# Attention scores of eight heads at once on parts of the array, in a kernel of attention, soft mixture of experts and a gated layer

## The chip, the cores and the metric
The kernel runs on one core of one Trainium2 chip. The metric is the device time of one execution in microseconds (us). The engines named below are TensorE (PE: matrix products; its weight loads are listed apart as PEld), VectorE (DVE), ScalarE (ACT), GpSimd (POOL) and SyncE (SP, which issues the DMAs).

## The reference, cut to what matters
All arrays are float32: 8 batches, 8 heads, 576 tokens, head size 64, 32 packing queries `p` per head.

```python
def sm_attn(qq, kk, vv):
    s = scale * (qq @ kk.T)
    a = exp(s - max(s)); a = a / (sum(a) + 1e-9)
    return a @ vv
p_packed = sm_attn(p, k, v)            # 32 x 64 per head
out = sm_attn(q, p_packed, p_packed)   # 576 x 64 per head
x = out, tokens x (heads * 64)         # 4608 x 512
# soft mixture of experts: logits = x @ phi (32 slots), softmax over tokens
# (dispatch) and over slots (combine); eight experts relu(s @ w1) @ w2
# gated layer: (sigmoid(x @ w_gate) * (x @ w_val)) @ w_out
```

## The kernel before, in words
The host lays `q` and `k` out by pairs of heads: 128 rows are the 64 head elements of two heads, and there are four pairs, j = 0 to 3. So row half r of pair j belongs to head 2j + r.

The attention stage (lines 107 to 526) runs a software pipeline over the eight batches. Iteration i of the loop at line 522 does the steps of the list `order`, each on batch i - lag: on batch i the packing scores (`scores`), their exponentials' transposes (`scores_tail`, `scores_t`) and the product with v (`pack`); on batch i - 1 the query scores (`pack_t`, `query`, `query_t`); on i - 2 to i - 4 the second softmax's sums, the attention's transposes, the slot logits with their running maximum, and the products that collect the slots (`dispatch`, `dispatch_t`, `slots_in`). Iterations 4 to 7 hold all lags; 0 to 3 fill the pipeline, 8 to 11 empty it.

The scores of both kinds are made by `heads_mm` (line 188). One call takes four heads (g = 0 or 1): two pairs, two halves of 288 tokens. The stationary operand is 128 rows by 64 columns: the packing queries of both heads of a pair in a block-diagonal layout with zeros (tiles `ptd` and `ppt`), so that one product gives two heads' scores. The two pairs of a call lie on two column parts of the array (`tile_position` (0, 0) and (0, 64)). The result goes to one buffer `sp` of two PSUM banks; the pool `p_big` has two such buffers, used by calls in turn. `scores` takes the maximum on VectorE (line 210) and the exponential with its sum on ScalarE (211); `query` copies the block to `s2`, group 0 on VectorE (the name s20 is in `ON_VECTOR`), group 1 on ScalarE. `packing` (157) writes the scaled block-diagonal `ptd` for the next batch on GpSimd.

Transposes go to PSUM buffers of the pool `p_tr` (two), the small products to `p_sm` (two). A step that needs a buffer waits until the last reader of its previous content is through.

What sets the order: the framework's planner orders every engine's instructions of the attention stage by its own costs, with the order of the text as priority, so TensorE's calls can be cut by others. The later stages are written with `keep_in_program_order` (class `Ordered`, line 550), which pins an engine's instruction behind the one written before it.

Loads go through SP's queue in order: p, then k, v, q of each batch, then the expert weights `wt` into 14 slots as these come free. The rest of the expert weights goes to slots that come free after the attention stage. The experts (line 732 on) begin with products that need `prun`, the attention's last result, and the gated layer follows.

Of the kernel before, what the change touches and what calls it, by code (L numbers as in the profile page):

```python
# [44 lines left out]
ON_VECTOR = {"m2", "s20"}  # L45
# [3 lines left out]
def kernel(  # L49
# [22 lines left out]

    ident = const.tile([128, 128], F32, name="ident")
    make_identity(nc, ident)
    i4 = const.tile([128, NS], F32, name="i4")
    masks = const.tile([128, 2, 2], F32, name="masks")
    nc.gpsimd.memset(masks, 0.0)
    for q in range(4):
        r = slice(32 * q, 32 * q + 32)
        nc.gpsimd.tensor_copy(out=i4[r, :], in_=ident[r, r])  # L80
        nc.gpsimd.memset(masks[r, 0, q % 2 : q % 2 + 1], 1.0)
        nc.gpsimd.memset(masks[r, 1, q // 2 : q // 2 + 1], 1.0)
# [19 lines left out]
    a4 = att.enter_context(tc.tile_pool(name="a4", bufs=4))  # L102
# [6 lines left out]
    ptds = [a1.tile([128, 4, 2, NP], F32, name=f"ptd{i}") for i in range(2)]  # L109
    phi = a1.tile([128, 4, NS], F32, name="phi")  # L110
    for t in ptds:
        nc.gpsimd.memset(t, 0.0)
# [44 lines left out]
    def packing(b):  # L157
        for r in range(2):
            rows = slice(64 * r, 64 * r + 64)
            (nc.gpsimd if b else nc.vector).tensor_scalar_mul(  # L160
                out=ptds[b % 2][rows, :, r, :], in0=praw[rows, b], scalar1=0.125
            )

    nc.sync.dma_start(out=praw, in_=pd)
    packing(0)
    for b in range(B):
        load(kt, b, kd[b], "kt")
        if b == 0:
            nc.sync.dma_start(out=phi, in_=phid)
        load(vt, b, vd[b], "vt")  # L170
        load(qt, b, qd[b], "qt")
# [16 lines left out]
    def heads_mm(dst, lhs, rhs, g):  # L188
        for n in range(2):
            for i in range(2):  # L190
                j = 2 * g + i
                nc.tensor.matmul(  # L192
                    dst[64 * i : 64 * i + 64, n, 0:HS],
                    lhsT=lhs[:, j].rearrange("p r k -> p (r k)"),
                    rhs=rhs[:, S * j + HS * n : S * j + HS * n + HS],
                    start=True,
                    stop=True,
                    tile_position=(0, 64 * i),
                )

    def scores(b, g):
        w = st.setdefault(b, {})
        if g == 0:
            w["nmax"] = a2.tile([128, 2], F32, name="nmax")
            w["ssum"] = a2.tile([128, 2], F32, name="ssum")
            w["e1"] = a1.tile([128, 2, S], F32, name="e1")
        sp = p_big.tile([128, 2, 512], F32, name="sp", tag="big")
        heads_mm(sp, ptds[b % 2], kt[b], g)
        nm = w["nmax"][:, g : g + 1]
        nc.vector.tensor_reduce(out=nm, in_=sp[:, :, 0:HS], axis=AX.XY, op=ALU.max, negate=True)  # L210
        nc.scalar.activation(  # L211
            w["e1"][:, g, :].rearrange("p (n s) -> p n s", n=2),
            sp[:, :, 0:HS],
            AF.Exp,
            bias=nm,
            accum_out=w["ssum"][:, g : g + 1],
        )
        if g == 1 and b + 1 < B:
            packing(b + 1)

    def scores_t(b, g):
        w = st[b]
        if g == 0:
            w["e1t"] = a1.tile([128, 8, 128], F32, name="e1t")
        tp = p_tr.tile([128, 4, 128], F32, name="tp", tag="tr")
        for c in range(4):
            nc.tensor.transpose(tp[:, c, :], w["e1"][:, g, 128 * c : 128 * c + 128], ident)
        copy(f"e1t{g}", w["e1t"][:, 4 * g : 4 * g + 4, :], tp)

    def scores_tail(b):  # L230
        w = st[b]
        e1, ssum = w["e1"], w["ssum"]
        tp = p_tr.tile([128, 4, 128], F32, name="tp", tag="tr")
        nc.tensor.transpose(tp[:, 0, :], e1[:, 1, 448:S], ident)
        nc.tensor.transpose(tp[0:64, 0, :], e1[:, 0, 512:S], ident)
        for g in range(2):
            rows = slice(64 * g, 64 * g + 64)
            copy(f"etail{g}", etail[rows, g, :], tp[rows, 0, :])
        nc.gpsimd.tensor_scalar_add(out=ssum, in0=ssum, scalar1=EPS)
        rs = a2.tile([128, 2], F32, name="rs")  # L240
        nc.vector.reciprocal(out=rs, in_=ssum)
        rsm = w["rsm"] = a2.tile([128, 2, 2], F32, name="rsm")
        nc.gpsimd.tensor_tensor(
            out=rsm,
            in0=rs[:, :, None].to_broadcast([128, 2, 2]),
            in1=masks[:, 0:1, :].to_broadcast([128, 2, 2]),
            op=ALU.mult,
        )

    def pack(b):  # L250
        w, v = st[b], vt[b]
        pq = p_sm.tile([128, 512], F32, name="pq", tag="sm")
        for g in range(2):
            for c in range(5):
                for q in range(4):
                    d0 = 64 * (4 * g + q)
                    if c < 4:
                        lhs, rhs = w["e1t"][:, 4 * g + c], v[:, DM * c + d0 : DM * c + d0 + 64]
                    else:
                        lhs, rhs = etail[:, g], v[:, 4 * DM + 64 * q : 4 * DM + 64 * q + 64]  # L260
                    nc.tensor.matmul(
# [7 lines left out]

        pp = w["pp"] = a4.tile([128, 2, 2, D], F32, name="pp")  # L270
        nc.vector.tensor_tensor(
            out=pp,
            in0=pq[:, 0:128].rearrange("p (g d) -> p g d", g=2)[:, :, None, :].to_broadcast([128, 2, 2, D]),
            in1=w["rsm"][:, :, :, None].to_broadcast([128, 2, 2, D]),
# [3 lines left out]
    def pack_t(b):  # L278
        w = st[b]
        pq = p_sm.tile([128, 512], F32, name="pq", tag="sm")  # L280
        for g in range(2):
            nc.tensor.transpose(pq[:, 128 * g : 128 * g + 128], w["pp"][:, g].rearrange("p r d -> p (r d)"), ident)
        ppt = w["ppt"] = a2.tile([128, 4, 2, NP], F32, name="ppt")
        copy("ppt", ppt.rearrange("p j r k -> p (j r k)"), pq[:, 0:256])

    def pack_phi(b):
        w = st[b]
        pq = p_sm.tile([128, 512], F32, name="pq", tag="sm")
        for j in range(4):
            g, i = j // 2, j % 2  # L290
            nc.tensor.matmul(
                pq[64 * i : 64 * i + 64, NS * g : NS * g + NS],
                lhsT=w["ppt"][:, j].rearrange("p r k -> p (r k)"),
                rhs=phi[:, j],
                start=True,
                stop=True,
                tile_position=(0, 64 * i),
# [4 lines left out]
    def query(b, g):  # L302
        w = st[b]
        if g == 0:
            w["s2"] = a1.tile([128, 2, S], F32, name="s2")
        sp = p_big.tile([128, 2, 512], F32, name="sp", tag="big")
        heads_mm(sp, w["ppt"], qt[b], g)
        copy(f"s2{g}", w["s2"][:, g, :].rearrange("p (n s) -> p n s", n=2), sp[:, :, 0:HS])

    def query_t(b, *parts):  # L310
        w = st[b]
        tps = []
        for c0, nch in parts:
            tp = p_tr.tile([128, 16, NP], F32, name="tp", tag="tr")
            for ci in range(nch):
                t0 = TOK[c0 + ci]
                for g in range(2):
                    h0 = 8 * ci + 4 * g
                    nc.tensor.transpose(  # L319
# [33 lines left out]
    def attn_t(b, part):  # L353
# [5 lines left out]
        if part < 2:  # L359
            for c in range(4):  # L360
                nc.tensor.transpose(tp[:, c, :], w["a"][:, c, 128 * part : 128 * part + 128], ident)
            copy(f"at{part}", at[:, part, 0:512].rearrange("p (c t) -> p c t", c=4), tp)
        else:
            for g in range(2):
                nc.tensor.transpose(tp[:, g, :], w["a"][:, 4, 128 * g : 128 * g + 128], ident)
            copy("at2", at[:, :, 512:S], tp[:, 0:2, 64:128])

    def logits(b):
        w = st[b]
        lp = p_sm.tile([128, 512], F32, name="lp", tag="sm")  # L370
        for g in range(2):
            for c in range(4):
                nc.tensor.matmul(
# [7 lines left out]
        for g in range(2):  # L381
            nc.tensor.matmul(
# [14 lines left out]
    def logits_t(b):  # L397
# [3 lines left out]
        nc.tensor.transpose(lt[:, 0:128], ls[:, 0:128], ident)  # L401
        nc.tensor.transpose(lt[:, 128:160], ls[0:32, 128:256], ident[0:32, 0:32])
        nc.tensor.transpose(lt[:, 256:384], cm.to_broadcast([128, 128]), ident)
# [18 lines left out]
    def dispatch(b):  # L422
        w = st[b]
        tps = p_sm.tile([128, 512], F32, name="tps", tag="sm")
        for c in range(4):
            nc.tensor.matmul(
# [8 lines left out]
        for c in range(4):  # L435
            n = slice(64 * c, 64 * c + 64 + c // 3)
            nc.tensor.matmul(
# [14 lines left out]
    def dispatch_t(b):  # L452
        w = st[b]
        tt = p_tr.tile([128, 512], F32, name="tt", tag="tr")
        for g in range(2):
            nc.tensor.matmul(
# [3 lines left out]
        tts = w["tts"] = a2.tile([128, 2, 2, NS], F32, name="tts")  # L460
        nc.vector.tensor_tensor(
            out=tts,
            in0=tt[:, 0 : 2 * NS].rearrange("p (g s) -> p g s", g=2)[:, :, None, :].to_broadcast([128, 2, 2, NS]),
            in1=masks[:, 1:2, :, None].to_broadcast([128, 2, 2, NS]),
# [11 lines left out]
    def slots_in(b):  # L476
        w = st.pop(b)
        pps = p_sm.tile([128, 512], F32, name="pps", tag="sm")
        for k in range(4):
            g = k // 2  # L480
            nc.tensor.matmul(
                pps[32 * k : 32 * k + 32, 0:128],
                lhsT=w["tts"][:, g, k % 2, :],
                rhs=w["pp"][:, g].rearrange("p r d -> p (r d)"),
                start=True,
                stop=True,
                tile_position=(0, 32 * k),
            )
# [6 lines left out]

    order = [
        (0, scores, 0),
        (3, attn_t, 1),
        (1, pack_t),
        (2, query_sum, (0, 2)),  # L500
        (3, attn_t, 2),
        (2, query_t, (4, 1)),
        (2, query_sum, (2, 2)),
        (0, scores, 1),
        (0, scores_tail),
        (0, scores_t, 0),
        (4, dispatch),
        (1, query, 0),
        (3, logits),
        (1, query, 1),  # L510
        (4, dispatch_t),
        (3, logits_t),
        (0, scores_t, 1),
        (2, query_sum, (4, 1)),
        (2, pack_phi),
        (1, query_t, (0, 2)),
        (1, query_t, (2, 2)),
        (4, slots_in),
        (0, pack),
        (2, attn_t, 0),  # L520
# [27 lines left out]


    class Ordered:  # L550
        def __init__(self, engine):
            self.engine = engine

        def __getattr__(self, name):
            op = getattr(self.engine, name)
            return lambda *args, **kw: tc.keep_in_program_order(op(*args, **kw))  # L556

    pe, act, dve, pool = [Ordered(e) for e in (nc.tensor, nc.scalar, nc.vector, nc.gpsimd)]
# [513 lines left out]
```

## Time and profile before

| | us |
|---|---|
| median of 3 runs | 568.49 (565.71 to 568.69) |
| the profiled execution | 568.5 |
| its span, first to last instruction | 566.7 |
| mean granted TensorE clock | 0.988 |

The span is the time from the first to the last instruction of the profiled execution; 1.8 us of its device time lie around it. The clock is the share of full speed that TensorE was granted.

### The profile page before, as it was taken

The numbers are of one execution on the slowest core, as the hardware profiler recorded it, in microseconds if no ns is written. First come the engines' busy times: TensorE is split into PE (matmuls) and PEld (weight loads), VectorE is DVE, ScalarE is ACT, GpSimd is POOL, SyncE is SP. The second block draws the span as 40 slices with busy tenths as digits, with TensorE's granted clock in tenths as the row PEclk, the third lists the DMA queues.
The fourth block names the chain that finished last, engine by engine and source line by source line (L and its number), as shares of the span: only waits on it lengthen the run. The fifth ranks groups of instructions, "written<-read, shape, count | busy, mean of one in ns | idle before, by whom it ended". The sixth has DMA issues, their size and how long they took to land.

```text
span 566.7 us, 10833 instructions
## 1 busy us (share of the span) xinstructions
PE 534.4 (94%) x4177; PEld 407.3 (72%) x4177; DVE 345.0 (61%) x846; ACT 292.6 (52%) x749; POOL 52.2 (9%) x131
## 2 busy tenths in 40 slices
PE   3889999997989799999999999999999999999997
PEld 1556666655555567787688888888888888888885
DVE  1377777783446478988989456567444644464444
ACT  2356555542356478897695444444444544454443
POOL 4132221230010000111011000000000000000000
PEclk9899999996999999999999999999999999999999
DMA  8999999931998656235200002022000200020002
GB/s 350 423 419 418 421 419 421 361 129 53 391 418 338 242 223 223 92 132 224 75 1 1 2 10 102 0 113 113 0 1 0 112 1 2 0 112 1 1 1 112
DMA packets 18099, 91.46 MB, mean 161 GB/s; under 512 B 1792, under 2 KB 2176, under 8 KB 11520
## 3 DMA queue, kind: packets, MB, share of 16 engines
q1 hardware_dynamic: 18048, 90.77, 40.6%
q8 instruction: 33, 0.54, 0.4%
q14 instruction: 18, 0.15, 0.1%
HBM read 81.33 MB, written 9.44 MB: 160 GB/s over the span
## 4 chain that ended last, share of the span: by engine, by line
PE 64%; DVE 3%; ACT 2%; DMA 2%; issue 1%; DVEq 0%
PE o_ps L556 50%; PE qg L556 11%; PE so_ps L556 2%; DMA wt<-in_w_dram 2%; PE qa L556 1%; ACT wgv L556 1%; DVE u L556 1%; DVE gv L556 1%; DVE held L556 0%; ACT gh L556 0%; ACT gv L556 0%; DVE gst L556 0%; DVE gl L556 0%; DVE wl L556 0%; ACT cst L556 0%
## 5 line engine op out<-in xcount | busy, mean ns | idle before, releaser
L556 PE MATMUL o_ps<-wh,gh 128*128 128x512 f32 x432 | 171.4, 397 | 1.6 <-DVE held L556 0.8
L556 PE MATMUL o_ps<-wl,gh 128*128 128x512 f32 x432 | 170.6, 395 | 0.0
L556 DVE TENSOR_TENSOR gv<-gv,qg 128x256 f32<-128x256 f32 x216 | 90.6, 419 | 131.2 <-ACT gv L556 130.4
L556 PE MATMUL o_ps<-wh,gl 128*128 128x512 f32 x432 | 168.3, 390 | 0.0
L556 ACT ACTIVATE gv<-qg 128x256 f32<-128x256 f32 x216 | 82.9, 384 | 155.7 <-PE qg L556 155.7
L556 PEld LDWEIGHTS qg<-cst,gst 128*128 128x128 f32 x432 | 79.5, 188 | 24.3 <-DVE gv L556 5.2
L556 PEld LDWEIGHTS o_ps<-wh,gl 128*128 128x128 f32 x432 | 81.2, 188 | 18.8 <-DVE gl L556 0.3
L556 PEld LDWEIGHTS o_ps<-wh,gh 128*128 128x128 f32 x432 | 81.1, 188 | 13.3 <-ACT gh L556 2.2
L556 DVE TENSOR_TENSOR gl<-gv,gh 128x256 fp32r<-128x256 f32 x216 | 90.5, 419 | 0.2
L556 PE MATMUL qg<-cst,gst 128*128 128x256 f32 x432 | 87.7, 285 | 2.6 <-DVE gv L556 1.6
L556 ACT CAST gh<-gv 128x256 fp32r<-128x256 f32 x216 | 86.6, 401 | 6.8 <-DVE gv L556 6.1
L556 PEld LDWEIGHTS o_ps<-wl,gh 128*128 128x128 f32 x432 | 81.9, 190 | 8.9
L192 PE MATMUL sp<-kt,ptd 128*64 128x288 f32 x128 | 23.2, 443 | 7.5 <-DMA kt<-in_k_dram 7.5
L556 ACT ACTIVATE wgv<-wgv 128x1024 f32<-128x1024 f32 (+3 forms) x28 | 28.3, 1021 | 0.0
L346 POOL TENSOR_TENSOR a<-ex,sm 128x512 f32<-128x512 f32 (+1 forms) x24 | 21.6, 904 | 67.9 <-DVE sm L345 49.6
L556 POOL CAST gst<-gst 32x128 fp32r<-32x128 f32 x40 | 13.5, 339 | 136.9 <-issue 66.1
L331 ACT ACTIVATE ex<-ex 128x512 f32<-128x512 f32 (+1 forms) x24 | 13.3, 560 | 16.9 <-DVE ex L328 16.9
L192 PE MATMUL sp<-qt,ppt 128*64 128x288 f32 x128 | 19.1, 419 | 1.7 <-ACT e L211 1.7
L192 PEld LDWEIGHTS sp<-kt,ptd 128*64 128x64 f32 x128 | 9.7, 145 | 14.6 <-issue 11.2
L324 DVE TENSOR_REDUCE mx<-tp 128x16 f32<-128x512 f32 (+1 forms) x24 | 14.2, 597 | 8.1 <-PE tp L319 7.6
L211 ACT ACTIVATE e<-sp,nmax 128x576 f32<-128x576 f32 x16 | 11.9, 745 | 13.2 <-DVE nmax L210 13.1
L556 PE MATMUL so_ps<-wt,htz 128*32 128x256 f32 x256 | 17.0, 384 | 1.1 <-DVE htz L556 1.0
(154 smaller groups left out, 575.4 us busy)
## 6 DMA issues: line engine op xcount, KB each, us to landing
wt<-in_w_dram SPq DMA_DIRECT2D x26, 1152.0 KB, 10.5
kt<-in_k_dram SPq DMA_DIRECT2D x8, 1152.0 KB, 22.3
vt<-in_v_dram SPq DMA_DIRECT2D x8, 1152.0 KB, 22.3
qt<-in_q_dram SPq DMA_DIRECT2D x8, 1152.0 KB, 22.4
out_dram<-os SPq DMA_DIRECT2D x35, 256.0 KB, 2.1
wgv<-in_wg_dram SPq DMA_DIRECT2D x5, 1024.0 KB, 7.0
wgv<-in_wv_dram SPq DMA_DIRECT2D x5, 1024.0 KB, 7.7
wo<-in_wo_dram SPq DMA_DIRECT2D x5, 1024.0 KB, 5.0
```

Of the source, the lines that this page charges most:

```text
L192: nc.tensor.matmul(dst[64 * i : 64 * i + 64, n, 0:HS], lhsT=lhs[:, j].rearrange("p r k -> p (r k)"), rhs=rhs[:, S * j + HS * n : S * j + H ...
L211: nc.scalar.activation(w["e1"][:, g, :].rearrange("p (n s) -> p n s", n=2), sp[:, :, 0:HS], AF.Exp, bias=nm, accum_out=w["ssum"][:, g : g ...
L324: nc.vector.tensor_reduce(out=mx[:, 0:n], in_=tp[:, 0:n, :], axis=AX.X, op=ALU.max)
L331: nc.scalar.activation(ex, ex, AF.Exp, scale=0.125)
L346: nc.gpsimd.tensor_tensor(out=w["a"][:, c0 : c0 + nch, 0:256].rearrange("p c (h k) -> p c h k", k=NP), in0=exs[c0][:, 0:n, 0:NP].rearrange ...
L556: return lambda *args, **kw: tc.keep_in_program_order(op(*args, **kw))
```

## The change
`heads_mm` now makes the scores of all eight heads in one call. A matmul takes one head: 64 rows (row half r) by 32 columns (part j), so eight parts of the array hold eight heads; the heads of row half r go to buffer r of two `sp` buffers, both taken by the call. With that the heads are grouped by their place in the pair (r) and no longer by halves of the list. The zero-padded `ptd`, `packing` and the masked `rsm` go; `p` is scaled in place once; `phi` is laid out with zeros, in two DMAs after a memset; `pp` and `ppt` have half the columns; `tts` has twice the columns, `slots_in` eight narrower products instead of four; `scores_tail` has four transposes instead of two. The copy s20 moves to ScalarE. Every TensorE instruction of the stage is pinned to the written order, and `order` is rewritten; VectorE, ScalarE and GpSimd stay with the planner. `room` only keeps the addresses of later tiles.

```diff
-ON_VECTOR = {"m2", "s20"}
+ON_VECTOR = {"m2"}
...
+    pe, act, dve, pool = [Ordered(e) for e in (nc.tensor, nc.scalar, nc.vector, nc.gpsimd)]
...
-    a4 = att.enter_context(tc.tile_pool(name="a4", bufs=4))
+    a4 = att.enter_context(tc.tile_pool(name="a4", bufs=5))
...
+    phi = a1.tile([128, 4, 2, NS], F32, name="phi")
+    nc.gpsimd.memset(phi, 0.0)
+    a1.tile([128, 384], F32, name="room")
...
-    packing(0)
+    nc.vector.tensor_scalar_mul(out=praw[:, 0], in0=praw[:, 0], scalar1=0.125)
+    nc.gpsimd.tensor_scalar_mul(out=praw[:, 1:B], in0=praw[:, 1:B], scalar1=0.125)
...
-    def heads_mm(dst, lhs, rhs, g):
-        for n in range(2):
-            for i in range(2):
-                j = 2 * g + i
-                nc.tensor.matmul(
-                    dst[64 * i : 64 * i + 64, n, 0:HS],
-                    lhsT=lhs[:, j].rearrange("p r k -> p (r k)"),
-                    rhs=rhs[:, S * j + HS * n : S * j + HS * n + HS],
...
-                    tile_position=(0, 64 * i),
+    def heads_mm(dst, lhs, rhs):
+        for n in range(2):
+            for j in range(4):
+                for r in range(2):
+                    rows = slice(64 * r, 64 * r + 64)
+                    pe.matmul(
+                        dst[r][32 * j : 32 * j + 32, n, 0:HS],
+                        lhsT=lhs[rows, j, :],
+                        rhs=rhs[rows, S * j + HS * n : S * j + HS * n + HS],
...
+                        tile_position=(64 * r, 32 * j),
...
+        sps = [p_big.tile([128, 2, 512], F32, name="sp", tag="big") for _ in range(2)]
+        heads_mm(sps, praw[:, b], kt[b])
+        for g, sp in enumerate(sps):
...
+            pe.transpose(tp[:, g, :], e1[:, g, 448:S], ident)
+            pe.transpose(tp[0:64, g, :], e1[:, g, 512:S], ident)
...
     order = [
-        (0, scores, 0), (3, attn_t, 1), (1, pack_t), (2, query_sum, (0, 2)),
-        (3, attn_t, 2), (2, query_t, (4, 1)), (2, query_sum, (2, 2)),
-        (0, scores, 1), (0, scores_tail), (0, scores_t, 0), (4, dispatch),
-        (1, query, 0), (3, logits), (1, query, 1), (4, dispatch_t),
-        (3, logits_t), (0, scores_t, 1), (2, query_sum, (4, 1)),
-        (2, pack_phi), (1, query_t, (0, 2)), (1, query_t, (2, 2)),
-        (4, slots_in), (0, pack), (2, attn_t, 0),
+        (0, scores), (4, dispatch), (1, pack_t), (3, attn_t, 1),
+        (2, query_sum, (0, 2)), (2, query_sum, (2, 2)), (3, attn_t, 2),
+        (2, query_t, (4, 1)), (1, query), (3, logits), (2, pack_phi),
+        (4, dispatch_t), (0, scores_tail), (0, scores_t, 0),
+        (0, scores_t, 1), (3, logits_t), (2, query_sum, (4, 1)),
+        (0, pack), (4, slots_in), (2, attn_t, 0),
+        (1, query_t, (0, 2)), (1, query_t, (2, 2)),
     ]
```

## Rows read from the trace of the kernel before

**Rows 1.** The page: busy time of each engine, share of the span, instructions.

```profile
PE 534.4 (94%) x4177; PEld 407.3 (72%) x4177; DVE 345.0 (61%) x846; ACT 292.6 (52%) x749; POOL 52.2 (9%) x131
```

**Rows 2.** Windows of the attention stage, every engine; the heading names the columns.

```profile
core 0: us, PE busy (x) PEld busy (x) DVE busy (x) ACT busy (x) POOL busy (x), PEclk, DMA share, GB/s
7.47:18.27 10.80, 8.10 (x108) 5.45 (x108) 2.11 (x4) 3.35 (x8) 1.47 (x4) 0.84 1.01 423
18.27:29.54 11.27, 9.69 (x144) 5.92 (x144) 5.94 (x11) 5.68 (x13) 1.47 (x4) 1.00 1.01 420
29.54:41.10 11.56, 10.37 (x149) 6.50 (x145) 7.99 (x19) 6.28 (x15) 4.15 (x7) 1.00 1.02 422
41.10:53.14 12.04, 11.81 (x171) 7.38 (x170) 9.20 (x21) 7.19 (x20) 4.18 (x7) 1.00 1.01 418
...
57.07:71.65 14.58, 14.57 (x205) 9.08 (x204) 10.35 (x29) 8.22 (x23) 4.24 (x9) 1.00 1.02 423
...
101.04:111.93 10.89, 10.73 (x185) 7.37 (x184) 8.13 (x22) 6.06 (x17) 1.22 (x5) 1.00 0.93 359
111.93:119.78 7.85, 7.85 (x88) 4.68 (x87) 5.85 (x21) 3.46 (x12) 2.82 (x4) 1.00 0.59 197
119.78:128.54 8.76, 7.30 (x86) 4.56 (x82) 8.12 (x25) 5.26 (x15) 2.71 (x3) 1.00 0.20 82
128.54:137.76 9.22, 6.40 (x79) 3.53 (x79) 3.48 (x15) 2.04 (x9) 0.00 (x0) 0.75 0.01 2
```

**Rows 3.** Timeline of TensorE, 67.38 to 72.6: start, us, what.

```profile
67.39 1.19 PE L192 MATMUL sp<-kt,ptd 128*64 128x288 f32 x8
68.51 0.66 PE L361 MATMUL tp<-ident,a 128*128 128x128 f32 x4
...
69.53 0.70 PE L192 MATMUL sp<-kt,ptd 128*64 128x288 f32 x2
70.16 0.44 PE L319 MATMUL tp<-ident,s 128*128 128x128 f32 x2
70.53 1.19 PE L192 MATMUL sp<-kt,ptd 128*64 128x288 f32 x6
71.65 0.64 PE L426 MATMUL tps<-a,ee 128*32 128x257 f32 x8
...
72.46 0.46 PE L192 MATMUL sp<-qt,ppt 128*64 128x288 f32 x2
```

**Rows 4.** Timeline of all engines, 136.5 to 138.5.

```profile
138.22 0.58 PE L556 MATMUL qa<-i 128*128 128x128 f32 x1 [0.47 <-DVE prun L490]
138.33 0.33 SPq L143 DMA_DIRECT2D wt<-in_w_dram  x1
```

**Rows 5.** Windows of line 192 alone (the head products).

```profile
67.38:67.68 0.30, 0.29 (x2) 0.20 (x4) 1.00 1.02 430
```

**Rows 6.** Groups by shape in 67.39 to 81.97: busy us, mean ns.

```profile
L211 ACT ACTIVATE e<-sp,nmax 128x576 f32<-128x576 f32 x2 | 1.5, 756 | 0.0
L210 DVE TENSOR_REDUCE nmax<-sp 128x1 f32<-128x576 f32 x2 | 1.5, 754 | 0.2 <-PE sp L192 0.2
L324 DVE TENSOR_REDUCE mx<-tp 128x16 f32<-128x512 f32 x2 | 1.4, 692 | 0.3 <-PE tp L319 0.2
L328 DVE TENSOR_TENSOR ex<-tp,mx 128x512 f32<-128x512 f32 x2 | 1.3, 681 | 0.0
...
L186 ACT COPY at<-tp 128x512 f32<-128x512 f32 x2 | 1.2, 576 | 0.7 <-PE tp L361 0.7
L186 ACT COPY s<-sp 128x576 f32<-128x576 f32 x1 | 0.6, 638 | 0.5 <-PE sp L192 0.5
...
L186 ACT COPY etail<-tp 64x128 f32<-64x128 f32 x2 | 0.5, 259 | 1.0 <-PE tp L235 1.0
L211 ACT ACTIVATION_READ_ACCUMULATOR e<-sp,nmax 128x1 f32 x2 | 0.4, 213 | 0.0
```

More of the change, by code (lines that the diff above doesn't have):

```diff
@@ L168 @@
         if b == 0:
-            nc.sync.dma_start(out=phi, in_=phid)
+            for r in range(2):
+                rows = slice(64 * r, 64 * r + 64)
+                nc.sync.dma_start(out=phi[rows, :, r, :], in_=phid[rows])
         load(vt, b, vd[b], "vt")
@@ L201, in scores @@
-    def scores(b, g):
-        w = st.setdefault(b, {})
[L203 to L219, printed above, removed]
+            for j in range(4):
+                for r in range(2):
+                    rows = slice(64 * r, 64 * r + 64)
+                    pe.matmul(
+                        dst[r][32 * j : 32 * j + 32, n, 0:HS],
+                        lhsT=lhs[rows, j, :],
+                        rhs=rhs[rows, S * j + HS * n : S * j + HS * n + HS],
+                        start=True,
+                        stop=True,
+                        tile_position=(64 * r, 32 * j),
+                    )
@@ L280, in pack_t @@
         pq = p_sm.tile([128, 512], F32, name="pq", tag="sm")
[L281 to L284, printed above, removed]
+        pe.transpose(pq[:, 0:128], w["pp"].rearrange("p r d -> p (r d)"), ident)
+        ppt = w["ppt"] = a2.tile([128, 4, NP], F32, name="ppt")
+        copy("ppt", ppt.rearrange("p j k -> p (j k)"), pq[:, 0:128])
     def pack_phi(b):
@@ L300, in pack_phi, with query @@
         copy("m2", m2.rearrange("p g s -> p (g s)"), pq[:, 0 : 2 * NS])
-    def query(b, g):
+    def query(b):
         w = st[b]
[L304 to L308, printed above, removed]
+        w["s2"] = a1.tile([128, 2, S], F32, name="s2")
+        sps = [p_big.tile([128, 2, 512], F32, name="sp", tag="big") for _ in range(2)]
+        heads_mm(sps, w["ppt"], qt[b])
+        for g, sp in enumerate(sps):
+            copy(f"s2{g}", w["s2"][:, g, :].rearrange("p (n s) -> p n s", n=2), sp[:, :, 0:HS])
     def query_t(b, *parts):
@@ L496 @@
     order = [
-        (0, scores, 0),
+        (0, scores),
+        (4, dispatch),
+        (1, pack_t),
         (3, attn_t, 1),
-        (1, pack_t),
         (2, query_sum, (0, 2)),
+        (2, query_sum, (2, 2)),
         (3, attn_t, 2),
         (2, query_t, (4, 1)),
-        (2, query_sum, (2, 2)),
-        (0, scores, 1),
+        (1, query),
+        (3, logits),
+        (2, pack_phi),
+        (4, dispatch_t),
         (0, scores_tail),
         (0, scores_t, 0),
[L507 to L511, printed above, removed]
+        (0, scores_t, 1),
         (3, logits_t),
-        (0, scores_t, 1),
         (2, query_sum, (4, 1)),
-        (2, pack_phi),
+        (0, pack),
+        (4, slots_in),
+        (2, attn_t, 0),
         (1, query_t, (0, 2)),
         (1, query_t, (2, 2)),
-        (4, slots_in),
-        (0, pack),
-        (2, attn_t, 0),
     ]
```

137 lines of the change are left out of this document (63 added, 74 removed).

## The prediction
> **What bounds the kernel now.** I read the page first: TensorE is busy for 534.4 of 566.7 us, VectorE for 345.0, ScalarE for 292.6 [rows 1]. That is a mean over stages, so the windows come next, cut where an iteration's score products start (up to 53.14) and, from 57.07, where its dispatch products start [rows 2]. In a full iteration (three such windows, 57.07 to 101.04, 14.5 to 14.8 us each) TensorE is busy for 14.57 of 14.58 us at a granted clock of 1.00, VectorE for 10.35, ScalarE for 8.22. The transfers run at a share of 1.0 there, but TensorE waits for none: they run ahead into the expert weights, and from 111.93 they thin out to 0.59, 0.20 and 0.01. So in the attention stage TensorE's own stream is the bound. Third, the timeline of one iteration [rows 3], which shows how that stream is cut: blocks of one array shape behind each other. Fourth, the end of the stage [rows 4]: the experts' first product waits for the last `prun`, and the weight transfers that had stopped start again beside it, at 138.33. So what the stage gains, all behind it gains: 138.22 to 566.7 us is carried over unchanged, and so are the 1.8 us between span and profiled time (568.5, which is the median too).
>
> **Step 1, the head products.** A call of heads_mm took 1.12 us (67.39 to 68.51) [rows 3]. Its four matmuls show as eight passes (x8) on two column parts, so four rounds. From the transposes between the calls: eight take 1.02 us (68.51 to 69.53), two take 0.37 (70.16 to 70.53), so one costs 0.11 and a block of a new shape 0.15; a round is then (1.12 - 0.15) / 4 = 0.24 us. Afterwards a call has 16 matmuls, 32 passes, on eight parts: four rounds again, for eight heads and not four. I add 0.05 for starting eight parts: 1.17 us. Two calls a batch in place of four: 4.48 - 2.34 = 2.14 us saved. That two column parts run at once is in these rows; that two row halves do is in none. Bounds: eight rounds a call if the halves take turns (2.1 us, nothing saved), or 2.24 saved if the start is free. I take the column parts' behaviour, the nearest row.
>
> In the rows the weight load of a part's next pass is not held up: in the first 0.30 us of a call two passes began and four loads were already done [rows 5]. The Trainium skill (TensorE: Matmul & The Clock Gate, Part 3, "The mechanism") says that loads overlap running matmuls only where the row group differs; by it each later round would wait for its load, which is rival D. The trace contradicts it here.
>
> **Step 2, the written order.** The second score call was cut by two transposes: 69.53 to 71.65 less their 0.37 is 1.75 us, 0.63 more than a whole call. That goes. Besides the head calls the iteration has 14 blocks of one shape in the timeline (attn_t with pack_t, query_t three times, dispatch in two shapes, logits twice, scores_tail with scores_t, dispatch_t to the second scores_t, pack_phi, slots_in twice, the second with pack, attn_t 0); the new order has 7 (dispatch on 128 rows, dispatch on 64, nine transposes, logits with pack_phi, the transposes from dispatch_t to logits_t, pack with slots_in, the last twelve transposes). 7 x 0.15 = 1.05 us saved. Small edits cancel: pack_t loses a transpose (-0.11), scores_tail gains two (+0.22), pack_phi runs on four parts instead of two (0 to -0.2), slots_in has the same columns in more pieces. TensorE's own work: 14.57 - 2.14 - 0.63 - 1.05 = 10.75 us.
>
> **Step 3, the other engines.** VectorE loses the copy s20 (some 0.7 us; pp halves, tts doubles): about 9.8 us. ScalarE gains it (0.64): 8.8. Both stay under 10.75, so no total becomes the bound; the chains between the engines do, because a call now takes both score buffers at once and TensorE may no longer go round a wait.
>
> **Step 4, walking one full iteration.** T = 0 is the start of the score products, done at 1.2.
> - VectorE still has the maximum and subtraction of the last two query_t blocks (0.69, 0.68; one each 0.6 when queued [rows 6]). The second block's transposes end at 0, so VectorE is through at 1.9. Then two score maxima of 0.75 (0.67 apart): 2.6 and 3.3.
> - ScalarE: the exponentials of the scores take 0.76 and 0.21 for the sum: 2.7 to 3.6, and 3.6 to 4.4 when both buffers are free. On the same queue lie the query exponential (0.63), ts, ppt, and the copy at1 (0.58), which must be out before query_t(4,1) finds its buffer; those transposes stand ahead of the query products. Behind the score exponentials that makes 5.3 to 5.7, ahead of some 4.6.
> - TensorE alone would reach the query products at 3.1: 1.17, dispatch 0.81 (71.65 to 72.46), nine transposes 1.1. So it waits for 1.5 to 2.6 us; I take 2.1. All behind it on TensorE waits too; nothing can fill the hole.
> - After the query products ScalarE has s20 and s21 (0.64 each), the ls copies and two etail (0.26 each) ahead of e1t, while TensorE needs only some 1.5 us to come to the second scores_t: 0.2 us of waiting. The last query_t block needs at0's buffer (0.58 behind four transposes, 0.44 of other work): 0.3 us more.
> An iteration is 10.75 + 2.1 + 0.5 = 13.4 us (12.4 with the short chain, 14.5 if the copies queue badly).
>
> **Step 5, the sum.** Steady part: from the first full iteration's scores (53.14) to the first dispatch without scores (111.93) are 58.79 us. The new order puts dispatch right after scores, so these are four iterations: 4 x 13.4 = 53.6, -5.2. Start, against rows 2: iteration 0 (10.80, clock 0.84) -2.0, an estimate: one call of two goes (1.1 us, more at the lower clock), and the next scores no longer stand behind pack_t's wait for pp. For the others the walk of step 4 is repeated with the steps that they have: iteration 1 (11.27) has no backlog of query reductions, so the query products go at 3.8, and 9.7 in all, -1.6; iteration 2 (11.56) has the backlog, query products at 4.4, 11.0, -0.6; iteration 3 (12.04) has the at copies too, 12.3, +0.3. Drain: 7.85 becomes 8.0 (+0.1, one query call saved against the strict order); 8.76, of which TensorE is idle 1.46, -1.5; the last 9.22 is a chain of dispatch and copies, 0. The new phi zeroing and second phi DMA on SP's queue lie in the 7.47 us in which TensorE waits for the first keys; nothing. Scaling p on GpSimd once replaces scaling per batch, which was off the chain. Sum: -5.2 steady, -3.9 start, -1.4 drain: -10.5. 568.5 - 10.5 = 558.0 us.
>
> **Rivals.**
> A. The waits of step 4 don't come, because VectorE takes the score maxima ahead of the query reductions: an iteration is TensorE's 10.75. 58.8 - 43.0 = 15.8, start 6.5, drain 2.5: 544 us. For it: VectorE has 4 us to spare in each of these windows [rows 2]. Against: the two buffers, both filled by each call.
> B. The row halves take turns: 8 rounds a call. An iteration is 13.4 + 2 x 0.97 = 15.3 us, steady +2.6, start about +2.5 (each of three iterations loses 1.9 against the forecast), drain +0.9: 574 us, slower. It decides from about 0.7 us a call lost. For it: no row shows two row halves at once. Against: column parts do run at once.
> C. The chain is longer: at1, e1t and the score exponentials queue so that an iteration is 14.5 us. Steady -0.8, start -1.5, drain 0: 566 us. For it: VectorE and ScalarE follow their own order, which TensorE's written one doesn't know.
> D. The loads of a part's next pass wait until the running pass is through. A pair's loads take 0.1 us (0.20 for four [rows 5]); three later rounds in each of two calls make 0.6 a batch, 5 us over eight: 563. Against: the same row. The sentence of the Trainium skill in step 1 is for it.
>
> **How the numbers follow.** Forecast 0.59, A 0.18, C 0.12, B 0.07, D 0.04. The forecast's own range is 552 to 564 (the iteration 12.4 to 14.5, start and drain within 2). To hold eight times in ten it reaches into A and to C: 545 to 567; outside lie B and the far end of A. Within 0.5% (2.8 us, about what a measurement of this kernel can tell) lie most of C and the edge of the forecast: 0.10. Slower by more: B and a still longer chain, 0.08. Faster: 0.82.
>
> **What would show it.** Right: a call on eight parts near 1.2 us with 32 passes; windows of full iterations at 13 to 14 us in which TensorE, for the first time, waits before the query products for ScalarE's e or at; ScalarE near 9 us an iteration; the experts' first product near 128. Wrong: a call of 2 us (B), iterations under 12 (A) or over 14.3 (C), or an expert stage that does not begin earlier by what the attention stage saved.

## The result and the profile after

| | median of the runs shown | range | profiled execution | span |
|---|---|---|---|---|
| before | 567.91 us (8) | 565.71 to 568.98 | 568.5 | 566.7 |
| after | 573.01 us (8) | 570.16 to 576.68 | 570.5 | 568.7 |

The ratio is 1.0102, 95% interval 1.0063 to 1.0140: one per cent slower, where 558.0 us was forecast and 567 was the upper end. The two profiled executions are 2.0 us apart, and that is the stage: the experts' first product begins at 140.38 us (before 138.22 [rows 4]), and from it to the end are 428.3 us (before 428.5). Its row, from the timeline:

```profile
140.38 1.01 PE L79 MATMUL qa<-i 128*128 128x128 f32 x3 [0.47 <-DVE prun L487]
```

The other 3 us between the medians go with the granted clock: the mean clock of a run is 0.970 to 0.988 after and 0.984 to 0.994 before, and the slowest run after (576.68) has 0.970, the fastest (570.16) 0.988.

The page of after, engine line (answers to [rows 1]):

```profile
PE 519.8 (91%) x4505; PEld 400.6 (70%) x4505; DVE 339.2 (60%) x837; ACT 295.7 (52%) x757; POOL 45.5 (8%) x105
```

Windows of after, cut at the starts of the score products and, from 111.80, of the dispatch products (columns and cuts as in [rows 2]):

```profile
core 0: us, PE busy (x) PEld busy (x) DVE busy (x) ACT busy (x) POOL busy (x), PEclk, DMA share, GB/s
7.43:16.23 8.80, 6.95 (x124) 4.42 (x125) 1.58 (x3) 3.25 (x8) 0.22 (x1) 1.00 1.01 420
16.23:25.97 9.74, 7.40 (x173) 4.59 (x165) 2.50 (x6) 4.58 (x11) 0.22 (x1) 1.00 1.01 421
25.97:37.65 11.68, 8.72 (x180) 5.37 (x179) 7.50 (x18) 6.55 (x15) 2.89 (x4) 1.00 1.01 417
37.65:52.17 14.52, 12.34 (x210) 7.67 (x209) 8.75 (x21) 8.35 (x21) 2.93 (x4) 0.88 1.02 422
...
66.70:81.20 14.50, 11.91 (x245) 7.98 (x244) 10.32 (x28) 8.62 (x23) 3.04 (x5) 1.00 1.01 421
81.20:97.30 16.10, 13.52 (x245) 8.81 (x244) 10.47 (x28) 8.74 (x23) 3.05 (x5) 0.89 1.01 418
...
111.80:121.60 9.80, 7.98 (x121) 5.03 (x120) 8.07 (x23) 5.30 (x15) 2.78 (x4) 1.00 0.60 228
121.60:129.50 7.90, 5.47 (x80) 3.54 (x79) 6.89 (x23) 3.92 (x11) 2.40 (x3) 1.00 0.00 0
129.50:140.40 10.90, 7.43 (x102) 4.45 (x102) 4.01 (x16) 2.78 (x11) 0.32 (x1) 0.75 0.01 2
```

A full iteration is as long as before (14.5 us), with TensorE busy for 11.91 us in place of 14.57. Two of the iterations have a granted clock under 0.9 (the end of the stage is low in both kernels). Finer windows show the stretches at the lower of the two levels, 1.2 GHz:

```profile
42.80:46.20 3.40, 3.38 (x57) 1.85 (x58) 1.35 (x6) 1.50 (x3) 2.21 (x4) 0.51 1.01 420
...
87.20:90.60 3.40, 3.40 (x60) 2.00 (x44) 1.23 (x6) 1.95 (x5) 1.77 (x3) 0.50 1.03 422
```

TensorE's timeline in the full iteration at 66.70 (answers to [rows 3]), where its waits are seen:

```profile
66.72 1.20 PE L79 MATMUL sp<-kt,praw 64*32 64x288 f32 x32
67.86 0.89 PE L79 MATMUL tps<-a,ee 128*32 128x257 f32 x16
...
71.64 0.44 PE L79 MATMUL tp<-ident,s 128*128 128x128 f32 x2 [1.98 <-ACT at L192]
72.01 1.57 PE L79 MATMUL sp<-qt,ppt 64*32 64x288 f32 x32
73.50 0.79 PE L79 MATMUL lp<-at,m 128*32 128x128 f32 x19
...
74.86 1.98 PE L79 MATMUL tp<-ident,e 128*128 128x128 f32 x12
76.68 0.45 PE L79 MATMUL lt<-ident,ls 128*128 128x128 f32 x2
...
78.89 0.43 PE L79 MATMUL pps<-pp,tts 128*32 128x64 f32 x16 [0.26 <-ACT lall L192]
...
80.64 0.66 PE L79 MATMUL tp<-ident,s 128*128 128x128 f32 x4 [0.29 <-ACT at L192]
```

The score call is 1.14 us from its start to the next (66.72 to 67.86), in 32 passes. The waits named are 1.98, 0.26 and 0.29 us. Two more hide in busy time: the query call takes 1.49 us (72.01 to 73.50), 0.35 more than the score call, and the twelve transposes take 1.82 us, 0.35 more than 12 x 0.11 + 0.15.

The loads and passes of the score call, from the view of the tile sp (answers to [rows 5]):

```profile
L79 PEld LDWEIGHTS sp<-kt,praw x32: 102/106/107, 66.7 to 67.3; 64*32 64x32 f32 x32
L79 PE MATMUL sp<-kt,praw x32: 402/403/427, 66.7 to 67.5; 64*32 64x288 f32 x32
```

The single operations kept their lengths (a score maximum takes 746 ns, before 754); one group by shape of 66.72 to 81.2 (busy us, mean ns; it answers to [rows 6]):

```profile
L192 ACT COPY at<-tp 128x512 f32<-128x512 f32 x2 | 1.2, 581 | 1.0 <-PE tp L79 1.0
```

And the chain of waits from 66.83 to the query products (start, length, what). It is new: in the window of before TensorE was busy for 14.57 of 14.58 us [rows 2].

```profile
66.83 0.69 DVE mx L321
67.52 0.61 DVE ex L325
...
68.22 0.64 ACT ex L328
...
68.88 0.70 DVE sm L338
69.58 0.68 DVE nmax L218
...
70.28 0.83 ACT e L219 x2
71.11 0.48 ACT at L192
...
71.64 0.44 PE tp L79 x2
72.08 1.50 PE sp L79 x32
```

The score products are done at 67.86, but VectorE's first score maximum begins 1.7 us later, behind the maxima, subtractions and one sum of the query block before; ScalarE then puts at1's copy behind the first score exponential, and TensorE stands before query_t(4,1) until it is out.

### The profile page after: what moved, and what is told of

Read it like the earlier page. It is cut to its first block, busy times and chain, and to the rows that moved or that the text cites. A ratio compares the mean times of both kernels' runs of the same rounds, so it can differ in the third digit from the quotient of the medians.

```text
span 568.7 us, 11438 instructions
## 1 busy us (share of the span) xinstructions
PE 519.8 (91%) x4505; PEld 400.6 (70%) x4505; DVE 339.2 (60%) x837; ACT 295.7 (52%) x757; POOL 45.5 (8%) x105
## 4 chain that ended last, share of the span: by engine, by line
PE 77%; DVE 9%; ACT 8%; DMA 3%; issue 2%; POOL 1%; SPq 0%; ACTq 0%; POOLq 0%; DVEq 0%
PE o_ps L79 50%; PE qg L79 11%; PE tp L79 5%; PE qa L79 3%; PE sp L79 3%; PE so_ps L79 2%; ACT e L219 2%; DMA wt<-in_w_dram 2%; PE pq L79 1%; ACT at L192 1%; DMA kt<-in_k_dram 1%; DVE ex L325 1%; PE lp L79 1%; DVE mx L321 1%; DVE nmax L218 1%
## 5 line engine op out<-in xcount | busy, mean ns | idle before, releaser
L79 PEld LDWEIGHTS o_ps<-wh,gl 128*128 128x128 f32 x432 | 81.2, 188 | 18.7 <-DVE gl L79 0.3
L328 ACT ACTIVATE ex<-ex 128x512 f32<-128x512 f32 (+1 forms) x24 | 13.2, 560 | 20.5 <-DVE ex L325 20.4
L79 PE MATMUL tp<-ident,s 128*128 128x128 f32 x80 | 13.4, 283 | 11.1 <-ACT at L192 10.9
L79 PE MATMUL tp<-ident,e 128*128 128x128 f32 x96 | 16.1, 302 | 3.8 <-ACT e L219 1.8
L79 PEld LDWEIGHTS tp<-ident,s 128*128 128x128 f32 x80 | 8.7, 141 | 14.7 <-ACT at L192 14.2
L79 PE MATMUL sp<-qt,ppt 64*32 64x288 f32 x256 | 14.7, 464 | 4.1 <-ACT e L219 3.9
L321 DVE TENSOR_REDUCE mx<-tp 128x16 f32<-128x512 f32 (+1 forms) x24 | 14.1, 590 | 6.2 <-PE tp L79 6.2
```

The lines of the kernel that those rows point to most:

```text
L321: nc.vector.tensor_reduce(out=mx[:, 0:n], in_=tp[:, 0:n, :], axis=AX.X, op=ALU.max)
L328: nc.scalar.activation(ex, ex, AF.Exp, scale=0.125)
```

## The experiments

Reasons to be told apart: that the written order by itself costs the time (W); that a call which takes both score buffers at once makes the wait in any order (P); that VectorE's own order is at fault (V); that a loop of waits through VectorE and ScalarE sets the iteration, so that each link taken out shortens it (L), against ScalarE's queue alone (Q). Where not said otherwise an edit is to the kernel after; ratios are to the kernel before, with 95% intervals. "Iteration" is a full one at clock 1.00.

**e1_free.** TensorE is left to the planner in the attention stage.

```
+    pe = nc.tensor            # in the attention stage only
```

> The changed kernel, but TensorE's order in the attention stage is left to the planner again; eight-part calls, buffers and layouts stay as changed. Theory W (the loss is TensorE waiting in its written order, 3.6 us in a 14.5 us iteration, mostly for the score exponentials and the copy at1 ahead of the query products): full iterations of 12 to 13 us and 558 to 563 us. Rival P (a call takes both score buffers, so the wait is there in any order): iterations of 14 to 14.5 and 568 to 573 us.

Measured: 569.24 us, 1.0009 (0.9978 to 1.0041). A full iteration, and pieces of TensorE's timeline in it:

```profile
68.40:82.60 14.20, 13.94 (x254) 8.73 (x248) 10.15 (x29) 8.46 (x23) 3.04 (x5) 1.00 1.01 422
```

```profile
71.94 1.90 PE L201 MATMUL sp<-qt,ppt 64*32 64x288 f32 x32
...
75.14 0.67 PE L201 MATMUL sp<-kt,praw 64*32 64x288 f32 x2
75.74 0.66 PE L234 MATMUL tp<-ident,e 128*128 128x128 f32 x4
```

From one dispatch to the next the full iterations take 14.7, 14.1 and 14.1 us (53.74 to 96.72), which is P's length. It is not P's wait: TensorE is busy for 13.94 of 14.20 us, and its stream is cut up. This query call takes 1.83 us (71.94 to 73.77) where 1.14 would do, and two passes of a score call, put ahead of the rest, take 0.60 us by themselves (75.14 to 75.74). Whether the planner cuts the calls because of the buffers is not shown. So the changed layout without the written order brings nothing measurable, although it removes two calls a batch; with the written order the time is 573.0 against 569.2.

**e2_oldpinned.** The kernel before with TensorE alone pinned to its text's order.

```
-    nc.tensor.matmul(...)     # and every transpose
+    pe.matmul(...)
```

> The kernel before, with nothing changed but that TensorE's instructions of the attention stage are pinned to its own written order. Theory W: pinning alone costs, since TensorE can no longer go round a wait: iterations of 15 to 16.5 us in place of 14.6, 573 to 583 us. Rival P: half calls leave one score buffer free, so pinning alone costs nothing: 566 to 570 us.

Measured: 581.63, 1.0236 (1.0194 to 1.0278); iteration 15.6. The longest waits of TensorE from 56.3 to 103:

```profile
PE tp L194 <- ACT e L221: 5.2, 3, 1.7
```

Rival P's 566 to 570 us is missed. A written order that doesn't suit the other engines costs 13.4 us in the old kernel (568.22 us beside it): W is true of an order, not of orders.

**e3_scoresfirst.** The scores ahead of attn_t 0 and the two query_t.

```
+    (3, attn_t, 0), (2, query_t, (0, 2)), (2, query_t, (2, 2)),   # after scores
-    (2, attn_t, 0), (1, query_t, (0, 2)), (1, query_t, (2, 2)),   # at the end
```

> The changed kernel with the written order turned by three steps: the score products stand ahead of attn_t 0 and the two large query_t steps, so that VectorE meets the score maxima before the query reductions and TensorE has 12 transposes more to do before the query products. Theory W: the wait before the query products shrinks from 2 us to under 0.5, full iterations of 12 to 12.5 us, 557 to 562 us. Rival P or a rival by which eight-part calls cost the clock: 568 to 573 us, iterations of 14 or more.

Measured: 568.81, 1.0013 (0.9994 to 1.0032). The iteration falls to 13.2, which neither theory had (12 to 12.5, and 14 or more); its waits are for the subtraction, the at copies and lall. But emptying the pipeline takes longer, 91.5 to 136.4 from the last scores on against 97.3 to 140.4 after (44.8 and 43.1).

**e4_fill.** Idle products in the wait before query_t(4,1).

```
+    for _ in range(7):
+        pe.matmul(fill[:, 0:128], lhsT=i16, rhs=i16, start=True, stop=True)
```

> The changed kernel with seven idle products (128x128, results not used) on TensorE ahead of query_t(4,1), where it waits for 2 us in iterations 2 to 7; about 1.5 us of work each. It adds work and takes nothing away. If the granted clock falls because of the wait (theory W): no half-clock stretch between 20 and 110 us, the mean clock at 0.985 to 0.988 in every run, and the time falls by 1 to 4 us against the changed kernel, 568.5 to 571. If it falls because eight-part calls leave the array thinly used (rival): half-clock stretches stay and the time is that of the changed kernel or up to 6 us longer, 573 to 579.

Measured: 576.30, 1.0144 (1.0128 to 1.0160). Windows of the stage and of its end:

```profile
24.90:130.70 105.80, 93.87 (x1740) 64.82 (x1738) 72.74 (x196) 58.23 (x155) 22.82 (x34) 1.00 0.88 362
...
130.70:144.60 13.90, 10.08 (x101) 6.18 (x101) 4.35 (x19) 3.47 (x13) 0.61 (x1) 0.50 0.01 1
```

In this trace the granted clock stays at 1.00 through all iterations with filled waits; one stretch at half the clock stands ahead of the first fill (21.5 to 24.9). So the low stretches of after come with the waits, as far as one trace shows it. It gains no time: the iterations grew to 14.7 to 15.3 (that the other engines' planned order changed with the new products is a guess), and the end of the stage ran at half the clock for longer.

**e5_apart.** The query products later, after logits, pack_phi and dispatch_t, over 4 us of work from the scores.

```
-    (1, query), (3, logits), (2, pack_phi), (4, dispatch_t),
+    (3, logits), (2, pack_phi), (4, dispatch_t), (1, query),
     # e3's steps go between scores and pack_t, attn_t 2 and query_t (4, 1) ahead of query_sum
```

> The changed kernel with another written order: the score products first, then attn_t 0, query_t(0,2), dispatch, query_t(2,2), pack_t, attn_t 1, attn_t 2, query_t(4,1), logits, pack_phi, dispatch_t, and only then the query products: over 4 us of TensorE's work lie between the two eight-part calls, in place of 2. Theory W (a call holds both score buffers until two maxima and two exponentials are through, some 4 us, and the written order had too little to put there): full iterations of 12 to 12.7 us, the wait before the query products gone, 561 to 566 us. Rival V (VectorE's planner-made order is the bound wherever the call stands): iterations of 13.2 or more as with the scores ahead of the query transposes, 567 to 570 us.

Measured: 577.83, 1.0148 (1.0105 to 1.0191): slower, against both. The buffer wait went, and others came (three full iterations wait 4.1 us for the query subtraction ex and 2.4 for etail). At clock 1.00 the iteration is 14.3 us, no longer than after; the extra time goes with the clock (mean 0.964 to 0.973; one full iteration has 17.8 us at 0.81), at the end of the stage too.

**e6_dve, e7_dveact, e8_apart_dve.** VectorE pinned to its text's order; ScalarE too; and VectorE with e5's order.

```
-    nc.vector.tensor_reduce(...)     # and all of VectorE in the stage
+    dve.tensor_reduce(...)           # e7: nc.scalar -> act as well
```

> The changed kernel with VectorE of the attention stage pinned to the order of the text too: maximum, subtraction, maximum, subtraction of the query blocks, then at once the two score maxima, with no sum of exponentials between. Rival V: the first score maximum starts 1.9 us after the score products in place of 2.8, full iterations of 13.4 to 13.8 us as the prediction's walk had it, 565 to 568 us. If ScalarE's queue (at1 behind the first score exponential) sets the wait: 14.2 to 14.6 us an iteration, 570 to 574 us.

> As the one before, with ScalarE pinned to the order of the text as well, so both score exponentials stand ahead of ts, ppt and at1. Rival V: within 1 us of the run with VectorE pinned alone. If ScalarE's queue sets the wait: query_t(4,1) waits longer for at1, 14.5 us an iteration or more, 571 to 577 us.

> The order with the two calls apart, and VectorE pinned to the order of the text. Theory W: the wait is gone already, so pinning VectorE moves it by under 2 us either way, 560 to 566. Rival V: 2 to 4 us faster than the same order with VectorE left to the planner.

Measured: 585.67, 1.0283 (1.0239 to 1.0326); 584.21, 1.0289 (1.0242 to 1.0336); 570.32, 1.0037 (1.0010 to 1.0063). In the text's order the wait for at is longer still (up to 2.2 and 2.3 us), and the iteration at clock 1.00 is 15.0 and 14.9 us, 0.4 to 0.5 over after, where V had 13.4 to 13.8. Most of the 12.7 and 11.2 us that they are slower than after goes with the clock: the mean is 0.956 to 0.959 in e6 and 0.953 to 0.968 in e7, whose one run at 0.978, the profiled one, took 574.23. With the products apart the same pin saves 7.5 us against e5, with an iteration of 13.8 and a clock of 0.975 to 0.984. V alone fails: no engine's order is good or bad without the others'.

**e9_short, e10_short_sm.** Three entries of the list `order` moved (the expectations call them four steps); then VectorE's query sums also kept behind what the text has before them.

```
-    (4, dispatch), (1, pack_t), (3, attn_t, 1),
+    (3, attn_t, 1), (4, dispatch), (1, pack_t),
-    (0, scores_t, 0), (0, scores_t, 1), (3, logits_t),
+    (0, scores_t, 0), (3, logits_t), (0, scores_t, 1),
-    (4, slots_in), (2, attn_t, 0),
+    (2, attn_t, 0), (4, slots_in),
     # e10: dve.tensor_reduce(out=sm[:, 0:n], ...) in query_sum
```

> After the change, with four steps of TensorE's written order moved: at1's transposes ahead of the dispatch products, the logits' transposes between the two blocks of score transposes, attn_t 0 ahead of slots_in. Theory L (a loop of waits through VectorE and ScalarE sets the iteration, and the written order decides which of them TensorE meets): the waits for lall (0.26), at0's copy (0.29), the etail copies (some 0.5) and part of at1 go, full iterations 13.0 to 13.5 us in place of 14.5, 565 to 569 us. Rival M (the loop does not care: shortened in one place, it waits in the next, since the other engines' planned orders follow along): iterations 14 to 15, 571 to 575 us.

> The same as the kernel with four steps moved, and the query softmax's sum reductions kept on VectorE behind what the text has before them, so that none goes ahead of a score maximum. Theory L: the first score maximum begins 0.6 us earlier, full iterations 12.5 to 13, 562 to 566 us. Rival M: 14 or more, 571 us or slower, as with VectorE wholly in written order (585.7).

Measured: 565.05, 0.9919 (0.9886 to 0.9951) and 563.97, 0.9896 (0.9863 to 0.9929). Both beat both kernels. An iteration and all its waits in e9:

```profile
67.80:81.20 13.40, 11.47 (x249) 7.82 (x248) 10.53 (x29) 8.24 (x23) 2.99 (x5) 1.00 1.01 421
```

```profile
PE sp L79 <- ACT ppt L192: 1.4, 1, 1.4
PE tp L79 <- DVE ex L325: 0.5, 1, 0.5
```

The waits for lall and at0 and the one for at1 are gone; one for ppt, behind the score exponentials on ScalarE, has come, and one for ex. L's size is met by e9. The sums kept behind bring nothing sure beyond (iteration 13.4 again, the intervals overlap).

**e12_nomax, e13_oldnomax.** Without the maxima of the query scores and their subtraction (the shift of the second softmax is left out), after and before.

```
-    nc.vector.tensor_reduce(out=mx[:, 0:n], ...); nc.vector.tensor_tensor(out=ex, ..., op=ALU.subtract)
-    nc.scalar.activation(ex, ex, AF.Exp, scale=0.125)
+    nc.scalar.activation(ex, tp[:, 0:n, :], AF.Exp, scale=0.125)
```

> After the change, without the maxima of the query scores and their subtraction: ScalarE takes the exponential straight from the transposes. Leaves out the shift of the second softmax by its maximum. VectorE loses about 3.2 us of its 10 in an iteration, TensorE nothing. Theory L (the loop of waits through VectorE is the bound now): the two links maximum 0.69 and subtraction 0.61 leave the loop and the score maxima begin near the end of the score products, so full iterations 11 to 12.5 us in place of 14.5, and 548 to 560 us. Rival O (the wait is TensorE's order and the score buffers, whatever VectorE does): iterations 13.8 to 14.5, 567 to 573 us.

> The kernel before the change with the same maxima and subtractions left out; its control. If TensorE's own stream is the bound there, VectorE's 3.2 us an iteration are worth nothing: iterations 14.4 to 14.8 us, 566 to 569 us. If waits on VectorE were a bound there too: iterations under 14 us, 560 us or less.

Measured: 564.69, 0.9898 (0.9858 to 0.9938) and 566.61, 0.9956 (0.9929 to 0.9983). A full iteration of each, e12 first:

```profile
64.60:78.50 13.90, 11.54 (x245) 7.79 (x244) 7.50 (x23) 8.54 (x23) 2.93 (x5) 1.00 1.01 420
```

```profile
71.20:85.30 14.10, 14.10 (x206) 8.97 (x206) 7.57 (x23) 7.83 (x22) 4.25 (x8) 1.00 1.01 421
```

Some 2.8 us of VectorE's work an iteration are worth 2.1 us to the whole kernel before, where TensorE works without a gap, and 8.3 us after. That agrees with a bound that the change moved off TensorE, but the totals say more than the iterations do. Before, two full iterations from dispatch to dispatch went from 14.6 and 14.8 to 14.0 and 14.8 us, with TensorE still busy throughout, and 1.9 of the 2.7 us by which the experts begin earlier in the profile (135.51 us) lie behind dispatch(4). After, each of four fell by 0.6; these 2.4 us, and 1.6 for a half-clock stretch in iteration 6 that e12's trace doesn't have, are most of the 5.9 us by which its experts begin earlier (134.46). So the iteration after fell only to 13.9, O's number, not L's 11 to 12.5, and the time lies between the two theories: TensorE still waits for at1, now behind ScalarE's own series.

```profile
67.07 0.74 ACT L219 ACTIVATE e<-sp,nmax 128x576 f32<-128x576 f32 x1
...
68.66 0.77 ACT L192 COPY at<-tp 128x512 f32<-128x512 f32 x2
```

**e15_at1, e16_nomax_short.** Of e9's moves that of attn_t 1 alone; and all of e9's moves with the part that e12 leaves out.

```
-    (0, scores), (4, dispatch), (1, pack_t), (3, attn_t, 1),     # e15
+    (0, scores), (3, attn_t, 1), (4, dispatch), (1, pack_t),
```

> After the change, with one step of TensorE's written order moved: at1's transposes ahead of the dispatch products. Theory Q (the wait is ScalarE's queue: at1's copy behind the exponentials of the scores): this move alone puts at1's copy ahead of them, the longest wait goes and the query products wait for ppt at most 1.4 us; full iterations 13.5 to 13.9 us and most of the gain of the four moves, 565 to 569 us. Rival L (the loop through VectorE sets the iteration; the moves that paid were those at lall, at0 and etail): 14.2 to 14.5 us, 570 to 573 us.

> Both remedies: the four moved steps, and the maxima and subtractions of the query scores left out (leaves out the shift of the second softmax). Theory Q and L as two loops, either of which is long enough by itself: neither wait is left, full iterations 11.5 to 12.5 us, near TensorE's 10.9, 550 to 560 us. Were ScalarE's queue the only bound, the four moves alone would have had all of it: 13.2 to 13.5 us, 562 to 565 us.

Measured: 572.80, 1.0086 (1.0062 to 1.0110) and 558.19, 0.9838 (0.9807 to 0.9869). The longest wait of an iteration of e15:

```profile
PE sp L79 <- ACT ppt L192: 1.6, 1, 1.6
```

Moving at1 exchanges a wait of 1.98 us for one of 1.6 at the next step, beside 0.3 each for ex, at and lall: the iteration is 14.2 us. So Q is out in the form tested, that at1's copy alone sets the time; ScalarE's queue is still in the wait, since ppt is a copy of ScalarE too. e9 differs from e15 by the moves of logits_t and attn_t 0, and these are worth the rest, 14.2 to 13.4 us.

The two remedies roughly add up: e9 is 8.0 us under after, e12 8.3, both together 14.8. So do the iterations: 1.1, 0.6 and, together, 1.7 us under 14.5 (12.8 there, over the 11.5 to 12.5 expected; 558.19 us is in the range). Two limits of which either is enough would not add; links of one loop do. That is argued from sums and not shown: the medians hold the end of the stage and the clock too, and e12's two links, 0.69 and 0.61 us, took only 0.6 us off the iteration.

**e14_packfirst, e11_s20.** e10 with pack_t at the front of the list; and after with the copy s20 back on VectorE.

```
+    (1, pack_t), (0, scores), (3, attn_t, 1), (4, dispatch),     # e14
-ON_VECTOR = {"m2"}
+ON_VECTOR = {"m2", "s20"}                                        # e11
```

> The kernel with four moved steps and the sums kept behind, with pack_t's transpose moved to the front of the list, so that the copy ppt is made before the exponentials of the scores. If the query products wait for ppt alone, 1.4 us an iteration go: 12.0 to 12.2 us, 555 to 559 us. If the wait behind it is the score buffers, which the second exponential frees at 71.25 in that kernel's trace while the products began at 71.74: 0.4 us an iteration, 12.9 to 13.1 us, 561 to 564 us. I expect the second.

> After the change, with the copy s20 (0.6 us) back on VectorE. It stood on no chain of waits in full iterations (ScalarE makes both copies at 73.70 to 74.88, ahead of transposes that come later): 571 to 575 us, iterations 14.3 to 14.7. If it matters (ls, etail and e1t queue behind it on ScalarE): 0.5 us an iteration less, 568 to 570 us; if VectorE suffers instead, 576 us or more.

Measured: 564.25, 0.9940 (0.9921 to 0.9960) and 573.71, 1.0115 (1.0068 to 1.0163). In e14 the wait for ppt is gone, and one for the score buffers is there:

```profile
PE sp L79 <- ACT e L219: 0.8, 1, 0.8
```

The full iterations are 12.8, 13.4 and 13.5 us: but for the first, not even the 0.4 us expected. In e11 the copy s20 makes no difference that shows over the spread of its runs (572.30 to 578.06).

Taken together: that the wait keeps its size in any order (P) is out, since e3 and e9 have iterations of 13.2 and 13.4 us with the same calls and buffers. The order written here did cost time (W), and so can others. VectorE's order alone (V) and at1's copy alone (Q) are out. A loop through VectorE and ScalarE (L) fits the rest best, but its size was wrong in e12 and its links were not told apart.

## Why the prediction was wrong

The stage by the terms of the sum, in the profiled execution (starts of windows):

| part | forecast | measured | miss |
|---|---|---|---|
| iterations 0 to 3 | 41.8 | 44.7 | +2.9 |
| four full iterations | 53.6 | 59.6 | +6.0 |
| from dispatch(4) to the experts | 24.9 | 28.6 | +3.7 |

Together 12.6 us, for the 12.5 between 558.0 forecast and 570.5 profiled.

- **Step 1 was right.** 1.17 us a call forecast, 1.14 measured, eight parts at once. Iterations 0 and 1 came out at 8.80 and 9.74 (forecast 8.8, 9.7); that iteration 0 agrees is in part luck, since its granted clock was 1.00, before 0.84, and the forecast gave no number for that. Rival B would have shown calls of 2.1 us, rival D of about 1.5. The rule that rival D rests on (the Trainium skill, TensorE: Matmul & The Clock Gate, Part 3, "The mechanism") does not show: the last load of the score call starts at 67.3, while passes run.
- **Step 4 failed, by 1.1 us an iteration.** Its large wait was nearly right (1.98 before query_t(4,1) and 0.35 in the query call, 2.3 against 2.1). Too small were TensorE's own work (14.5 less all five waits is 11.3, against step 2's 10.75; which of its terms fell short is not known) and the waits behind the query products: 0.35 for etail, 0.26 for lall, 0.29 for at0, 0.9 in all against 0.5. The walk took VectorE's and ScalarE's queues in an order that I chose. The planner's order differs: a query sum ahead of the first score maximum (68.88), at1 between the two score exponentials. With three entries moved (e9) these small waits are gone and the iteration is 13.4, the forecast's own number, though with other waits than the walk had.
- **The sum held the clock at 1.00.** The windows of before had shown a low clock where TensorE was idle in the first iteration and at the end, and the new waits of 2 us were not priced for it. Two stretches of 3.4 us at half the clock stand in iterations 3 and 6; iteration 6 is 1.6 us longer than its neighbours. In e4 no such stretch stands where the waits are filled. How large the term can get e5, e6 and most runs of e7 show, at mean clocks of 0.953 to 0.973.
- **Step 5 miscounted the drain.** Dispatch(4) is at the same time in both (111.93 and 111.80), but in the old list attn_t 1 and pack_t of that iteration stood ahead of it, in the new one behind. The steady part was credited with them and the drain not charged: the query call after it follows at 115.03 against 113.88, 1.15 us, and 0.69 us of the way to it are waits (TensorE's timeline, before and then after):

```profile
113.88 1.19 PE L192 MATMUL sp<-qt,ppt 128*64 128x288 f32 x8
```

```profile
113.35 1.01 PE L79 MATMUL tp<-ident,a 128*128 128x128 f32 x6 [0.40 <-DVE ex L325]
114.66 0.44 PE L79 MATMUL tp<-ident,s 128*128 128x128 f32 x2 [0.29 <-ACT at L192]
115.03 1.20 PE L79 MATMUL sp<-qt,ppt 64*32 64x288 f32 x32
```

The chain of the last batches then runs through one wait after another (ee 2.1 us, cm 1.1, at 1.2): from 111.5 us to the experts TensorE's waits sum to 7.5 us, before to 3.9, where the forecast had less idle time and not more. The last iteration takes a further 1.2 us (129.50 to 140.38 against 128.54 to 138.22), and 0.8 of it is the order again: six transposes of attn_t now stand between its dispatch products and its logits, which begin 1.6 us after the dispatch and not 0.8 (before and then after):

```profile
129.36 0.64 PE L373 MATMUL lp<-at,m 128*32 128x128 f32 x16
```

```profile
130.32 0.88 PE L79 MATMUL tp<-ident,a 128*128 128x128 f32 x6
131.13 1.16 PE L79 MATMUL lp<-at,m 128*32 128x128 f32 x20
```

e9, which puts attn_t 1 ahead of the dispatch products again, needs 41.7 us from the last scores to the experts, after 43.1. No run changes the drain alone.

- **Rival C** had the iteration (14.5 us) and the reason, but its 566 left the drain at zero and the clock out. The chance for slower, 0.08, was too small: every error of a walk through queues that nobody wrote down goes the same way, to more waiting.

So the expected gain was turned into waits. TensorE's 2.7 us less of busy time an iteration were given back: before, 14.5 us are its own stream, after, 11.3 us of work and 3.2 of waits. That the two agree is chance. The rest of the slowdown is the drain and the clock. Not settled is which link of the loop holds the iteration at 13.4 in e9, e10 and e14 alike, although the longest wait is for ppt in the first two and for the score buffers in the third.

## What to carry to other kernels

Work taken from a fully busy engine is worth at most the distance to the next limit, here waits on the other engines: look for that length first, with the buffers as the change will hold them. An order written for one engine has to be laid against the orders of the engines that feed it, wait by wait; here three moved entries were worth 8 us, more than the whole change lost. Price an engine's new idle time twice: as waiting, and as what the granted clock does after it.

## What the runs showed of the hardware

Products on 64-row by 32-column parts run on both row halves and all four column parts at once: 32 passes of 0.40 us each in 1.14 us. With TensorE waiting for about 2 us once in an iteration, the granted clock fell to half for 3.4 us in some iterations and not in others of the same shape; e11_s20 had one iteration of 17.2 us at a clock of 0.80 where its neighbour took 14.5 at 1.00:

```profile
52.50:67.00 14.50, 12.04 (x245) 8.05 (x244) 10.38 (x29) 8.18 (x22) 3.00 (x5) 1.00 1.01 419
67.00:84.20 17.20, 14.67 (x251) 10.18 (x252) 11.00 (x29) 8.20 (x22) 3.04 (x5) 0.80 1.01 421
```
